# One level of Strassen's scheme in the second product of a feed-forward block, one core of a Trainium2

## Chip, cores and metric

The kernel runs on one core of one Trainium2 chip. The metric is device time in microseconds (us) of one launch. All arithmetic on values is in 32-bit floats.

## The reference

An mLSTM cell over q, k, v, three gates (4 batches, 8 heads, 768 steps, head dimension 40) gives x with 3072 rows and 320 columns; a feed-forward block follows:

```python
def _moe_ref(x, w_in, w_out) -> np.ndarray:     # x (3072, 320), w_in (320, 2048), w_out (2048, 320)
    h = np.maximum(x @ w_in, 0.0)
    return (h * h @ w_out).astype(np.float32)
```

The weights come as 64-bit floats and are rounded on the chip to 32 bits.

## The kernel before, in words

The 3072 rows are 24 tiles of 128 (4 batches of 6 chunks), s = 0 to 23. For each tile an attention step runs: `transposes` (k and q turned on TensorE, L342; ScalarE copies kT, VectorE copies qT, L346), `scores` (L355), `weighted` (VectorE multiplies the scores by the weights W, giving P_sb, L367), `attend` (hi, dC and hp on TensorE, L378, L385, L392; VectorE and POOL carry the state C on), `normalise` (eight or nine short VectorE operations, L418 to L428, that use the sigmoid of o_gate), and `turn_rows` (L437, copied to xT by ScalarE, L438). `weigh` makes W for the next tile: POOL masks A_bc (L312), ScalarE takes eight exponentials (L318).

Four tiles make a group of 512 rows, g = 0 to 5. For each group the feed-forward block has two stages of eight units each. A unit of the first product, `ffn1(g, p)`, makes two of the 16 blocks of d_ff: 128 x 512 results in PSUM (L452, L457; three banks h_ps), the relu on ScalarE into one of four r_sb buffers (L460), the square on VectorE into g2 (L461). A unit of the second product, `ffn2(g, j, part)`, runs 8 of the 16 matmuls of one tile of 128 rows, with 128 x 128 of g2 as the stationary operand and 320 columns of w_out streaming (L509), into one of two banks o_ps; after the second half ScalarE copies the 128 x 320 results (L515) and SP's queue writes them out (L517). TensorE runs a 32-bit matmul as two records in the trace.

The order of the work is written out by hand, and every engine takes its instructions in that order. A first part handles tiles 0 to 5, the rounding of the weights (`Rounding`, with buffers in the pool conv) and the first product of group 0. Then a loop runs over n = 8 to 95, sixteen units to a group (u = n mod 16): each unit is one of `ffn1` or `ffn2`, and the attention step of tile s = 4 + n // 4 is laid between four of them: `score` at n mod 4 = 0, `attend_on` at 1 (with the loads of tile s + 4 and of o_gate), `weigh_on` for the next tile at 2, `turn_rows` and the next tile's `transposes` at 3. At s = 7 and s = 15 ScalarE also takes the sigmoids of the next eight tiles of o_gate. The last two pieces of w_out are rounded at n = 8. From n = 80 on (group 5) no attention is left.

Of the kernel before, what the change touches and what calls it, by code (L numbers as in the profile page):

```python
# [9 lines left out]
F32 = mybir.dt.float32  # L10
# [4 lines left out]
ALU = mybir.AluOpType  # L15
PSUM = bass.MemoryType.PSUM

P = 128
# [11 lines left out]
def kernel(  # L30
# [21 lines left out]

    nc = tc.nc
    B, H, S, D = q.shape
    BH = B * H
    NB = S // P
    NT = B * NB
    PR = H // 2  # L60
    DP = 64
    D1 = D + 1
    DM = H * D
    DFF = moe_w_in.shape[1]
    NF = DFF // P
    NPAIR = NF // 2
    GT = 4
    NG = NT // GT
    W = GT * P
# [2 lines left out]

    consts = ctx.enter_context(tc.tile_pool(name="consts", bufs=1))
    ld = ctx.enter_context(tc.tile_pool(name="ld", bufs=2))
    conv = ctx.enter_context(tc.tile_pool(name="conv", bufs=2))
    prep = ctx.enter_context(tc.tile_pool(name="prep", bufs=2))
    work = ctx.enter_context(tc.tile_pool(name="work", bufs=2))
    xts = ctx.enter_context(tc.tile_pool(name="xts", bufs=2))
# [2 lines left out]
    ps_o = ctx.enter_context(tc.tile_pool(name="ps_o", bufs=2, space=PSUM))  # L81
    ctx.enter_context(tc.manual_schedule())
    first = ExitStack()
    gates = first.enter_context(tc.tile_pool(name="gates", bufs=1))

    A_d = nc.dram_tensor("a_rows", (BH, S), F32, kind="Internal").ap()

# [12 lines left out]
    w_out = consts.tile([P, NF, DM], F32)  # L100
# [31 lines left out]
    pieces = []  # L132
# [81 lines left out]
    rounding = Rounding()  # L214
# [36 lines left out]
    st = {}  # L251


    RUNS = ((0, 2), (2, 4), (4, 8), (8, 16), (16, 24))

    def load_parts(s):
        d = st.setdefault(s, {})
# [8 lines left out]
    def load_o(s):  # L266
        b, c = divmod(s, NB)
        r, (s0, s1) = next((r, (a, z)) for r, (a, z) in enumerate(RUNS) if a <= s < z)
        if s == s0:
            st["og", r] = ld.tile([P, 8, H, D], F32, name="og")  # L270
        og = st.setdefault(s, {})["og"] = st["og", r][:, s - s0]
        nc.sync.dma_start(og, o_gate[b, :, c * P : (c + 1) * P, :].rearrange("h p d -> p h d"))

    def sigmoid(s):
        nc.scalar.activation(st[s]["og"], st[s]["og"], AF.Sigmoid)
# [95 lines left out]
    def attend(s):  # L371
        b, c = divmod(s, NB)
        d = st[s]
        C = st.get("C")
        if c > 0:
            hi = ps_at.tile([P, H, D1], F32, name="hi", tag="at")
            for j in range(PR):
                nc.tensor.matmul(  # L378
                    hi[:, 2 * j : 2 * j + 2, :].rearrange("p h d -> p (h d)"), lhsT=d["qT"][:, j, :],
                    rhs=C[:, j].rearrange("p h d -> p (h d)"), start=True, stop=True,  # L380
                )
        if c + 1 < NB:
            dC = ps_at.tile([P, PR, 2, D1], F32, name="dC", tag="at")
            for j in range(PR):
                nc.tensor.matmul(  # L385
                    dC[:, j].rearrange("p h d -> p (h d)"),
                    lhsT=d["kq"][:, 0, 2 * j : 2 * j + 2, :].rearrange("p h d -> p (h d)"),
                    rhs=d["vw"][:, 2 * j : 2 * j + 2, :].rearrange("p h d -> p (h d)"), start=True, stop=True,
                )
        hp = d["hp"] = ps_at.tile([P, H, D1], F32, name="hp", tag="at")  # L390
        for h in range(H):
            nc.tensor.matmul(  # L392
                hp[:, h, :], lhsT=d["P"][h % 2][:, h // 2, :], rhs=d["va"][:, h, :], start=True, stop=True,
            )
        d["num"] = hp
        if c > 0:
            num = d["num"] = work.tile([P, H, D1], F32, name="num")
            nc.vector.tensor_tensor(  # L398
                num[:], hi[:], eA_T[:, b, c, :].unsqueeze(2).to_broadcast([P, H, D1]), op=ALU.mult,
            )  # L400
        if c + 1 < NB:
            Cn = work.tile([P, PR, 2, D1], F32, name="C_sb")
            nc.vector.tensor_tensor(Cn[:], dC[:], bdm[:], op=ALU.mult)  # L403
            if c > 0:
                Cd = work.tile([P, H, D1], F32, name="Cd")
                nc.gpsimd.tensor_tensor(
                    Cd[:], C[:].rearrange("p j i d -> p (j i) d"),
                    d["dec"][:].unsqueeze(2).to_broadcast([P, H, D1]), op=ALU.mult,
                )
                Cf = Cn[:].rearrange("p j i d -> p (j i) d")  # L410
                nc.gpsimd.tensor_tensor(Cf, Cf, Cd[:], op=ALU.add)  # L411
            st["C"] = Cn
# [29 lines left out]
    def ffn1(g, p):  # L442
        if p == 0 and g > 0:
            st["g2"] = ffn.tile([P, NF, W], F32, name="g2", bufs=1)
        xT = st["xT", g]
        hs = []
        for i in range(2):
            fb = 2 * p + i
            h = ps_h.tile([P, W], F32, name="h_ps")
            hs.append(h)  # L450
            for a in range(2):
                nc.tensor.matmul(  # L452
                    h[:], lhsT=w_in[:, a, fb * P : (fb + 1) * P], rhs=xT[:, a, :], start=(a == 0), stop=False,
                )
        for i in range(2):
            rows = slice(i * KR, (i + 1) * KR)
            nc.tensor.matmul(hs[i][:], lhsT=w_in2[rows, p, :], rhs=xT[rows, 2, :], start=False, stop=True)  # L457
        for i in range(2):
            r = ffn.tile([P, W], F32, name="r_sb", bufs=4)
            nc.scalar.activation(r[:], hs[i][:], AF.Relu)  # L460
            nc.vector.tensor_tensor(st["g2"][:, 2 * p + i, :], r[:], r[:], op=ALU.mult)  # L461
# [42 lines left out]
    def ffn2(g, j, part):  # L504
        if part == 0:
            st["o_ps"] = ps_o.tile([P, W], F32, name="o_ps")[:, :DM]
        o_ps = st["o_ps"]
        for fb in range(part * NF // 2, (part + 1) * NF // 2):
            nc.tensor.matmul(  # L509
                o_ps, lhsT=st["g2"][:, fb, j * P : (j + 1) * P], rhs=w_out[:, fb, :],  # L510
                start=(fb == 0), stop=(fb == NF - 1),
            )
        if part == 1:
            y = ffn.tile([P, DM], F32, name="y_sb")
            nc.scalar.copy(y[:], o_ps)  # L515
            t = g * GT + j
            nc.sync.dma_start(out[t * P : (t + 1) * P, :], y[:])  # L517


    def do(f, s):  # L520
        if 0 <= s < NT:
            f(s)

    def weigh_on(s):
        do(weigh, s)
        do(load_A, s + 2)
# [5 lines left out]
    def attend_on(s):  # L532
        do(attend, s)
        do(normalise, s)
        do(load, s + 4)
        if 4 <= s < 8:
            load_o(2 * s)
            load_o(2 * s + 1)
        elif 8 <= s < 16:
            load_o(s + 8)  # L540


    zeros = consts.tile([P, W], BF16)
# [47 lines left out]
    ffn = ctx.enter_context(tc.tile_pool(name="ffn", bufs=2))  # L591
# [4 lines left out]
    sigmoid(0)  # L596
    sigmoid(1)
    attend(0)
    rounding.step()
    normalise(0)  # L600
    load_o(2)
    load_o(3)
    attend(1)
    normalise(1)
    rounding.step()
# [12 lines left out]
    for u in range(8):  # L618
        s = 2 + u // 2
# [37 lines left out]
    NU = NPAIR + 2 * GT  # L657
    assert NU == 4 * GT
    for n in range(NPAIR, NU * NG):
        g, u = divmod(n, NU)  # L660
        s, at = GT + n // 4, n % 4
        if at == 0:
            do(score, s)
        if at == 1:
            attend_on(s)
        if at == 3:
            do(turn_rows, s)
            do(transposes, s + 1)
            if s in (7, 15):
                for r in range(s + 1, s + 9):  # L670
                    sigmoid(r)
        if u < NPAIR:
            ffn1(g, u)
        else:
            ffn2(g, *divmod(u - NPAIR, 2))
        while rounding.done < len(pieces):
            rounding.step()
        if at == 2:
            do(weigh_on, s + 1)

# [29 lines left out]
```

## Time and profile before

| | |
|---|---|
| Times of three runs, median | 608.71 us (607.28 to 608.88) |
| The profiled execution's own time | 608.44 us |
| Its span, first to last instruction | 606.7 us |
| Mean granted TensorE clock | 0.989 |
| L509 (second product) on TensorE | 768 records, 213.8 us |
| L452 and L457 (first product) on TensorE | 480 records, 192.1 us |

The trace names engines PE (TensorE matmuls), PEld (TensorE weight loads, which can lie beside matmuls), DVE (VectorE), ACT (ScalarE), POOL (GpSimd) and SP (the queue that issues most transfers). A group of instructions is shown as: line, engine, operation, output <- inputs, shapes, count | busy us, mean ns of one | idle time of the engine just before them, and what ended it. Ends of matmuls are modelled, so the distance between their starts tells more than their busy time. The chain of waits is followed back from the last instruction to whatever released each piece; a row of it in order of time is start, length, engine, tile, line and count.

### The profile page before, as it was taken

Reading aid. Unit: us, or ns where it says so; the run is one execution under the profiler, and the core shown is the slowest. Engines: PE = TensorE matmul, PEld = TensorE weight load, DVE = VectorE, ACT = ScalarE, POOL = GpSimd, SP = SyncE. Lnnn points to the kernel's source line nnn. Section 1 sums busy time; section 2 is a strip of 40 time slices with the busy share of each in tenths; the row PEclk is TensorE's granted clock in tenths of the full one; section 3 lists DMA queues with packets and bytes.
Section 4 is the critical chain, followed back from the end, with each engine's and each line's share of the span. In section 5 each row is a group of like instructions: output and inputs, shape, how many; then the busy total and the mean of one; then the engine's idle time right before and its main releaser. Section 6 shows DMA issues by size and latency. Waiting matters only on the chain.

```text
span 606.7 us, 7558 instructions
## 1 busy us (share of the span) xinstructions
PE 592.3 (98%) x2870; PEld 389.3 (64%) x2871; DVE 239.6 (39%) x468; ACT 192.4 (32%) x476; POOL 95.9 (16%) x113
## 2 busy tenths in 40 slices
PE   9979897999999999999999999999999999999997
PEld 5868776777645677645577655477755477733575
DVE  7688989712334322235323144322143431113100
ACT  3757567123351321132320524410214312022100
POOL 3345444202101110101021010101010110000000
PEclk9988998999999999999999999999999999999999
DMA  9898899615212143133143123122201000000000
GB/s 197 206 184 200 158 199 222 102 59 100 46 44 43 37 88 66 50 61 58 35 90 55 56 34 66 37 59 51 70 1 36 0 1 23 11 11 2 0 23 22
DMA packets 130901, 42.47 MB, mean 70 GB/s; under 512 B 101073, under 2 KB 127697, under 8 KB 130865
## 3 DMA queue, kind: packets, MB, share of 16 engines
q1 hardware_dynamic: 130768, 41.79, 33.2%
q8 instruction: 23, 0.38, 0.3%
q10 hardware_dynamic: 96, 0.20, 0.1%
q14 instruction: 14, 0.11, 0.1%
HBM read 37.95 MB, written 4.03 MB: 69 GB/s over the span
## 4 chain that ended last, share of the span: by engine, by line
PE 89%; DVE 6%; ACT 2%; issue 1%; POOL 1%; POOLq 0%; DVEq 0%; ACTq 0%
PE o_ps L509 35%; PE h_ps L452 23%; PE h_ps L457 7%; PE hp L392 6%; PE tp L355 3%; PE tp L342 3%; PE dC L385 3%; PE hi L378 2%; PE h_ps L476 2%; PE tp L437 1%; DVE mag L194 1%; DVE mag L195 1%; ACT W_sb L318 1%; PE idle L549 1%; POOL A_bc L312 1%
## 5 line engine op out<-in xcount | busy, mean ns | idle before, releaser
L509 PE MATMUL o_ps<-w_out,g 128*128 128x320 f32 x768 | 213.8, 435 | 0.0
L509 PEld LDWEIGHTS o_ps<-w_out,g 128*128 128x128 f32 x768 | 143.5, 190 | 57.9 <-issue 0.8
L452 PE MATMUL h_ps<-xT,w_in 128*128 128x512 f32 x320 | 146.9, 602 | 0.0
L461 DVE TENSOR_TENSOR g<-r_sb 128x512 f32<-128x512 f32 x80 | 51.7, 688 | 147.8 <-ACT r_sb L460 147.8
L452 PEld LDWEIGHTS h_ps<-xT,w_in 128*128 128x128 f32 x320 | 57.7, 190 | 69.9 <-issue 65.2
L460 ACT ACTIVATE r_sb<-h_ps 128x512 f32<-128x512 f32 x80 | 43.4, 595 | 162.6 <-PE h_ps L457 162.5
L515 ACT COPY y_sb<-o_ps 128x320 f32<-128x320 f32 x24 | 10.2, 425 | 185.8 <-PE o_ps L509 185.8
L318 ACT ACTIVATE W_sb<-A_bc,b_T 128x128 f32<-128x128 f32 x176 | 53.7, 391 | 7.9 <-POOL A_bc L312 7.9
L329 POOL TENSOR_TENSOR vw<-va,W_sb 128x328 f32<-128x328 f32 x20 | 14.9, 743 | 211.2 <-ACT W_sb L318 205.3
L367 DVE TENSOR_TENSOR P_sb<-tp,W_sb 128x512 f32<-128x512 f32 x46 | 29.6, 684 | 45.1 <-PE tp L355 43.0
L392 PE MATMUL hp<-va,P_sb 128*128 128x41 f32 x368 | 45.7, 286 | 0.0
L457 PE MATMUL h_ps<-xT,w_in 64*128 64x512 f32 x160 | 45.2, 641 | 0.0
L392 PEld LDWEIGHTS hp<-va,P_sb 128*128 128x128 f32 x368 | 44.6, 198 | 0.0
L346 DVE COPY qT<-tp 128x512 f32<-128x512 f32 x23 | 15.8, 687 | 70.2 <-PE tp L342 70.2
L411 POOL TENSOR_TENSOR C_sb<-C_sb,Cd 128x328 f32<-128x328 f32 x16 | 14.5, 906 | 138.1 <-DVE C_sb L403 137.8
L476 PE MATMUL h_ps<-xT,w_in 128*128 128x256 f32 x128 | 33.1, 415 | 3.0 <-ACT r_sb L495 1.2
L457 PEld LDWEIGHTS h_ps<-xT,w_in 64*128 64x128 f32 x160 | 12.0, 184 | 30.3 <-issue 30.3
L476 PEld LDWEIGHTS h_ps<-xT,w_in 128*128 128x128 f32 x128 | 26.1, 210 | 8.1 <-ACT r_sb L495 1.6
L355 PEld LDWEIGHTS tp<-qT,kT 40*128 40x128 f32 x384 | 24.1, 187 | 10.8 <-issue 6.8
L342 PE MATMUL tp<-ident,kq 128*128 128x128 f32 x192 | 26.6, 283 | 3.3 <-DVE num L398 3.3
L355 PE MATMUL tp<-qT,kT 40*128 40x128 f32 x384 | 27.1, 280 | 0.8 <-DVE qT L346 0.8
L342 PEld LDWEIGHTS tp<-ident,kq 128*128 128x128 f32 x192 | 23.0, 147 | 4.5 <-DVE num L398 3.8
(82 smaller groups left out, 468.8 us busy)
## 6 DMA issues: line engine op xcount, KB each, us to landing
A_bc<-a_rows SPq DMA_DIRECT2D x22, 512.0 KB, 3.9
raw<-in_moe_w_out_dram SPq DMA_DIRECT2D x16, 320.0 KB, 4.1
raw<-in_moe_w_in_dram SPq DMA_DIRECT2D x8, 512.0 KB, 5.1
kq<-in_k_dram SPq DMA_DIRECT2D x24, 160.0 KB, 4.0
kq<-in_q_dram SPq DMA_DIRECT2D x24, 160.0 KB, 4.4
va<-in_v_dram SPq DMA_DIRECT2D x24, 160.0 KB, 4.1
og<-in_o_gate_dram SPq DMA_DIRECT2D x24, 160.0 KB, 4.0
out_dram<-y_sb SPq DMA_DIRECT2D x24, 160.0 KB, 1.8
```

The source lines that it names most:

```text
L318: nc.scalar.activation(d["W"][:, i * n + h, :], A[i][:, h, :], AF.Exp, bias=b_T[:, b, c, i * n + h : i * n + h + 1],)
L342: nc.tensor.transpose(tp[:, j, :], d["kq"][:, i, 2 * j : 2 * j + 2, :].rearrange("p h d -> p (h d)"), ident[:],)
L355: nc.tensor.matmul(sc[i][:, j, :], lhsT=d["kT"][rows, j, :], rhs=d["qT"][rows, j, :], start=True, stop=True,)
L367: nc.vector.tensor_tensor(t, d["sc"][i], d["W"][:].rearrange("p (j two) t -> p j two t", two=2)[:, :, i, :], op=ALU.mult,)
L385: nc.tensor.matmul(dC[:, j].rearrange("p h d -> p (h d)"), lhsT=d["kq"][:, 0, 2 * j : 2 * j + 2, :].rearrange("p h d -> p (h d)"), rhs=d[" ...
L392: nc.tensor.matmul(hp[:, h, :], lhsT=d["P"][h % 2][:, h // 2, :], rhs=d["va"][:, h, :], start=True, stop=True,)
L452: nc.tensor.matmul(h[:], lhsT=w_in[:, a, fb * P : (fb + 1) * P], rhs=xT[:, a, :], start=(a == 0), stop=False,)
L457: nc.tensor.matmul(hs[i][:], lhsT=w_in2[rows, p, :], rhs=xT[rows, 2, :], start=False, stop=True)
L460: nc.scalar.activation(r[:], hs[i][:], AF.Relu)
L461: nc.vector.tensor_tensor(st["g2"][:, 2 * p + i, :], r[:], r[:], op=ALU.mult)
L476: nc.tensor.matmul(hs[i][:, n, :], lhsT=w_in[:, a, fb * P : (fb + 1) * P], rhs=xT[:, a, cols], start=(n == 0 and a == 0), stop=False,)
L509: nc.tensor.matmul(o_ps, lhsT=st["g2"][:, fb, j * P : (j + 1) * P], rhs=w_out[:, fb, :], start=(fb == 0), stop=(fb == NF - 1),)
```

## The change

For groups 1 to 5 the second product of a group, (512 rows x 2048) times (2048 x 320), is cut in two along each of its three dimensions: rows into tiles {0, 1} and {2, 3}, d_ff into blocks of even and odd number, the columns of w_out into 160 and 160. In place of the eight block products, seven are made (Winograd's form): P1 = A11 B11, P2 = A12 B21, P3 = S4 B22, P4 = A22 T2 (with its sign turned), P5 = S1 T0, P6 = S2 T1, P7 = S3 (B22 - B12), where A is g2 and B is w_out. They run for tile pairs (0, 2) and (1, 3), four units each.

- `sums` (VectorE): S1, S2, S3 (in place of A21) and S4 for two of the eight pairs of blocks at a time, four operations of 512 elements a partition; called at u = 2, 4, 6 and 8.
- `sums_of_weights` (VectorE): T0, T1, T2 at n = 10, 12, 14, and B22 - B12 in place of B12 at n = 18; 1280 elements a partition each.
- `product`: eight matmuls of 160 columns. Two banks X and Y take products by turns, and some of the additions are made by accumulating onto a product that is still there.
- `ffn2_fast`: four steps for a pair; step 3 has one product, the others two. Two ScalarE copies and five VectorE additions of 128 x 160 empty the banks into two rows y, which go out at steps 2 and 3.
- Memory: the pool conv is closed after the rounding, and S and T (pool late) take its place; o_gate is loaded in runs of four tiles in place of eight, at s = 8 to 19 for tile s + 4, and its sigmoids are taken in batches of four at s = 7, 11, 15 and 19; num and Cd have one buffer each.

Group 0 keeps `ffn2`. The core of the diff:

```diff
-    conv = ctx.enter_context(tc.tile_pool(name="conv", bufs=2))
...
+    brought = ExitStack()
+    conv = brought.enter_context(tc.tile_pool(name="conv", bufs=2, side="right"))
...
-    RUNS = ((0, 2), (2, 4), (4, 8), (8, 16), (16, 24))
+    RUNS = ((0, 2), (2, 4)) + tuple((s, s + 4) for s in range(4, NT, 4))
...
-            st["og", r] = ld.tile([P, 8, H, D], F32, name="og")
+            st["og", r] = ld.tile([P, 4, H, D], F32, name="og")
...
-            num = d["num"] = work.tile([P, H, D1], F32, name="num")
+            num = d["num"] = work.tile([P, H, D1], F32, name="num", bufs=1)
...
-                Cd = work.tile([P, H, D1], F32, name="Cd")
+                Cd = work.tile([P, H, D1], F32, name="Cd", bufs=1)
...
+    DH = DM // 2
+    W2 = W // 2
+    wo = w_out[:].rearrange("p (f two) d -> p f two d", two=2)
+    B11, B12 = wo[:, :, 0, :DH], wo[:, :, 0, DH:]
+    B21, B22 = wo[:, :, 1, :DH], wo[:, :, 1, DH:]
+    T = {}
+
+    def sums_of_weights(i):
+        if i < 3:
+            T[i] = late.tile([P, NPAIR, DH], F32, name=f"T{i}", bufs=1)[:]
+        if i == 0:
+            nc.vector.tensor_tensor(T[0], B12, B11, op=ALU.subtract)
+        elif i == 1:
+            nc.vector.tensor_tensor(T[1], B22, T[0], op=ALU.subtract)
+        elif i == 2:
+            nc.vector.tensor_tensor(T[2], B21, T[1], op=ALU.subtract)
+        else:
+            nc.vector.tensor_tensor(B12, B22, B12, op=ALU.subtract)
+
+    def sums(p0):
+        if p0 == 0:
+            st["S"] = [late.tile([P, NPAIR, W2], F32, name=f"S{n}", bufs=1) for n in (1, 2, 4)]
+        S1, S2, S4 = (t[:, p0 : p0 + 2] for t in st["S"])
+        g4 = st["g2"][:].rearrange("p (f two) t -> p f two t", two=2)[:, p0 : p0 + 2]
+        A11, A12, A21, A22 = (g4[:, :, i, n * W2 : (n + 1) * W2] for n in range(2) for i in range(2))
+        nc.vector.tensor_tensor(S1, A21, A22, op=ALU.add)
+        nc.vector.tensor_tensor(S2, S1, A11, op=ALU.subtract)
+        nc.vector.tensor_tensor(A21, A11, A21, op=ALU.subtract)
+        nc.vector.tensor_tensor(S4, A12, S2, op=ALU.subtract)
+
+    def product(to, lhsT, rhs, start=False):
+        for p in range(NPAIR):
+            nc.tensor.matmul(
+                to, lhsT=lhsT[:, p], rhs=rhs[:, p, :], start=(start and p == 0), stop=(p == NPAIR - 1),
+                skip_group_check=True,
+            )
+
+    def ffn2_fast(g, i, step):
+        if step == 0:
+            banks = [ps_o.tile([P, W], F32, name="o_ps") for _ in range(2)]
+            st["o2"] = banks if i == 0 else banks[::-1], [ffn.tile([P, DM], F32, name="y_sb") for _ in range(2)]
+        (X, Y), (y0, y1) = st["o2"]
+        g4 = st["g2"][:].rearrange("p (f two) t -> p f two t", two=2)
+        cols = [slice((i + 2 * n) * P, (i + 2 * n + 1) * P) for n in range(2)]
+        S1, S2, S4 = (t[:, :, i * P : (i + 1) * P] for t in st["S"])
+        X1, X5, Y6 = X[:, :DH], X[:, DH : 2 * DH], Y[:, :DH]
+        add = lambda to, a, b: nc.vector.tensor_tensor(to, a, b, op=ALU.add)
+        m1, u12, u22 = y1[:, :DH], y0[:, DH:], y1[:, DH:]
+        if step == 0:
+            product(X1, g4[:, :, 0, cols[0]], B11, start=True)
+            nc.scalar.copy(m1, X1)
+            product(Y6, S2, T[1], start=True)
+            add(u12, Y6, m1)
+        elif step == 1:
+            product(X1, g4[:, :, 1, cols[0]], B21)
+            nc.scalar.copy(y0[:, :DH], X1)
+            product(Y6, g4[:, :, 0, cols[1]], B12)
+            add(u22, Y6, m1)
+        elif step == 2:
+            product(X5, S1, T[0])
+            add(u22, u22, X5)
+            product(Y6, g4[:, :, 1, cols[1]], T[2])
+            add(m1, m1, Y6)
+            t = g * GT + i + 2
+            nc.sync.dma_start(out[t * P : (t + 1) * P, :], y1[:])
+        else:
+            product(X5, S4, B22)
+            add(u12, u12, X5)
+            t = g * GT + i
+            nc.sync.dma_start(out[t * P : (t + 1) * P, :], y0[:])
...
-        if 4 <= s < 8:
-            load_o(2 * s)
-            load_o(2 * s + 1)
-        elif 8 <= s < 16:
-            load_o(s + 8)
+        if 8 <= s < 20:
+            load_o(s + 4)
...
+        if n == NPAIR + 1:
+            brought.close()
+            late = ctx.enter_context(tc.tile_pool(name="late", bufs=1, side="right"))
+        if u == NPAIR and g > 0:
+            sums(NPAIR - 2)
         if at == 0:
             do(score, s)
         if at == 1:
             attend_on(s)
+        if n in (NPAIR + 2, NPAIR + 4, NPAIR + 6, NU + 2):
+            sums_of_weights((n - NPAIR) // 2 - 1 if n < NU else 3)
+        if 0 < u < NPAIR and u % 2 == 0:
+            sums(u - 2)
         if at == 3:
             do(turn_rows, s)
             do(transposes, s + 1)
-            if s in (7, 15):
-                for r in range(s + 1, s + 9):
+            if s % 4 == 3:
+                for r in range(s + 1, min(s + 5, NT)):
                     sigmoid(r)
         if u < NPAIR:
             ffn1(g, u)
+        elif g == 0:
+            ffn2(g, *divmod(u - NPAIR, 2))
+            while rounding.done < len(pieces):
+                rounding.step()
         else:
-            ffn2(g, *divmod(u - NPAIR, 2))
-        while rounding.done < len(pieces):
-            rounding.step()
+            ffn2_fast(g, *divmod(u - NPAIR, 4))
```

## The prediction

> **What bounds the kernel now.** I read the page of the profile first: busy shares, the 40 slices, and the chain of work that ended last.
>
> ```profile
> PE 592.3 (98%) x2870; PEld 389.3 (64%) x2871; DVE 239.6 (39%) x468; ACT 192.4 (32%) x476; POOL 95.9 (16%) x113
> ...
> PE   9979897999999999999999999999999999999997
> ...
> DVE  7688989712334322235323144322143431113100
> ...
> PEclk9988998999999999999999999999999999999999
> ...
> PE 89%; DVE 6%; ACT 2%; issue 1%; POOL 1%; POOLq 0%; DVEq 0%; ACTq 0%
> PE o_ps L509 35%; PE h_ps L452 23%; PE h_ps L457 7%; PE hp L392 6%; PE tp L355 3%; PE tp L342 3%; PE dC L385 3%; PE hi L378 2%; PE h_ps L476 2%; PE tp L437 1%; DVE mag L194 1%; DVE mag L195 1%; ACT W_sb L318 1%; PE idle L549 1%; POOL A_bc L312 1%
> ```
>
> TensorE is busy for 98% of the span and is 89% of the chain; the largest entry, 35%, is the line that the change replaces, the second product L509. A busy TensorE may only be waiting with a matmul in flight, so I asked next for the stretches: the second table gives each engine's busy time (and instruction count) in a first-product stage, in a second-product stage, and in the last group.
>
> ```profile
> core 0: us, PE busy (x) PEld busy (x) DVE busy (x) ACT busy (x) POOL busy (x), PEclk, DMA share, GB/s
> 203.97:249.46 45.49, 45.49 (x240) 34.46 (x238) 11.88 (x25) 9.29 (x27) 4.75 (x5) 1.00 0.32 68
> 249.46:297.50 48.04, 48.04 (x210) 24.76 (x212) 18.06 (x36) 14.56 (x37) 4.79 (x6) 1.00 0.25 49
> 568.70:606.70 38.00, 34.63 (x128) 24.15 (x128) 1.29 (x2) 2.79 (x6) 0.00 (x0) 1.00 0.05 18
> ```
>
> The second-product stage of group 1 (the first row) has no idle TensorE at all, at a granted clock of 1.00, while VectorE works 11.88 of 45.49 us. Whether its time is really streaming shows in the pitch of its matmuls, which the chain in order of time gives (start, us, how many):
>
> ```profile
> 55.65 3.46 PE h_ps L476 x16
> ...
> 204.86 4.50 PE o_ps L509 x16
> ...
> 211.11 1.75 PE hp L392 x16
> ...
> 221.88 0.87 PE tp L342 x8
> 222.75 4.31 PE o_ps L509 x16
> ...
> 457.86 3.44 PE h_ps L452 x8
> 461.30 1.06 PE h_ps L457 x4
> ...
> 568.68 34.66 PE o_ps L509 x128
> ```
>
> A record of 512 columns takes 3.44/8 = 430 ns, one of 320 takes 4.31/16 = 269.4, one of 256 takes 3.46/16 = 216.3. The line through the first two is 0.836 ns per column and 1.8 ns; it gives 216 at 256, as measured. So these stages are bound by the columns streamed, and a stage that streams fewer columns ends earlier, as long as nothing else comes last. The floor on the other side is the weight load that every record brings: hp streams 41 columns only and still takes 1.75/16 = 109 ns, the transposes 0.87/8 = 109 ns.
>
> **The change, part by part.** The durations that its terms need stand in the groups of instructions (count, then busy us and mean ns):
>
> ```profile
> L509 PE MATMUL o_ps<-w_out,g 128*128 128x320 f32 x768 | 213.8, 435 | 0.0
> ...
> L461 DVE TENSOR_TENSOR g<-r_sb 128x512 f32<-128x512 f32 x80 | 51.7, 688 | 147.8 <-ACT r_sb L460 147.8
> L460 ACT ACTIVATE r_sb<-h_ps 128x512 f32<-128x512 f32 x80 | 43.4, 595 | 162.6 <-PE h_ps L457 162.5
> ...
> L515 ACT COPY y_sb<-o_ps 128x320 f32<-128x320 f32 x24 | 10.2, 425 | 185.8 <-PE o_ps L509 185.8
> ...
> L367 DVE TENSOR_TENSOR P_sb<-tp,W_sb 128x512 f32<-128x512 f32 x46 | 29.6, 684 | 45.1 <-PE tp L355 43.0
> ```
>
> *Removed.* L509 has 768 records: 24 row tiles, 16 blocks of d_ff, two records to a matmul. Five of six groups change: 640 records x 269.4 ns = 172.4 us, all on the path.
>
> *Added on TensorE.* Each of those groups has two pairs of row tiles, seven products each, 8 matmuls to a product, two records to a matmul: 2 x 7 x 8 x 2 = 224 records of 160 columns, 1120 in all. No row has 160 columns. The line above gives 0.836 x 160 + 1.8 = 135.6 ns. From below it is bounded by half of 269.4, 134.7; from above by a load that is not hidden at all, 109 + 134.7 = 244 ns. I take 135.6: the 256-column row lies on the line and the 109 ns floor is 26 ns under it, so the load still fits behind the stream. 1120 x 135.6 = 151.9 us, again all on the path. Difference: 172.4 - 151.9 = 20.5 us off.
>
> *Starts of products.* A start can cost more than the pitch: the x16 after the scores took 4.50 us, that after the transposes 4.31, so 0.19 us at the first start of a stage. Each group now has 14 products, each waiting for a bank to be emptied. A bank change in the old stage costs next to nothing (34.66 - 8 x 4.31 = 0.18 us over the whole last group, its first start included). Bounds: 0 and 14 x 5 x 0.19 = 13 us; I take 1 us, by the nearest row, the bank changes.
>
> *Emptying the banks.* Per pair two ScalarE copies of 160 columns and five VectorE additions with one operand in PSUM. From L515 (320, 425 ns) and L460 (512, 595) a copy of 160 is an estimated 283 ns. A PSUM operand on VectorE is in L367 and in the row below, 328 columns: 1.03 ns per column, so an estimated 322 ns at 160, 50 x 0.322 = 16 us.
>
> ```profile
> L398 DVE TENSOR_TENSOR num<-hi,eA_T 128x328 f32<-128x328 f32 x20 | 9.9, 495 | 29.4 <-PE hi L378 29.4
> ...
> L275 ACT ACT_TABLE_LOAD x5 | 6.4, 1283 | 0.1
> ```
>
> The banks alternate X, Y, X, Y: while one is emptied the other takes a product of 16 x 135.6 ns = 2.17 us, against 0.32 or 0.28 us of emptying, so the cost is nothing. The cover shrinks to nothing only if VectorE is over 1.8 us behind at that moment.
>
> *Block sums of g2.* Four tensor_tensor of 512 elements for every two pairs of blocks, 16 a group, 80 in all, 688 ns each by L461: 55 us of VectorE. Those of u = 2, 4, 6 stand in the first-product stage, where VectorE is busy 18.06 of 48.04 us; with 12 x 0.688 = 8.3 us it comes to 26. What queues behind them are the squares, which wait for the relu of the same unit, a whole unit (3.44 + 1.06 = 4.5 us) later; the four sums take 2.75. Cost nothing; without that cover the four r_sb buffers still let VectorE lag nearly two units. Those of u = 8 are the tight ones; the old course of that place, group 1, is:
>
> ```profile
> 203.80 1.06 PE L355 MATMUL tp<-qT,kT 40*128 40x128 f32 x16
> ...
> 204.63 1.29 DVE L461 TENSOR_TENSOR g<-r_sb 128x512 f32<-128x512 f32 x2 [3.96 <-ACT r_sb L460]
> 204.79 4.57 PE L509 MATMUL o_ps<-w_out,g 128*128 128x320 f32 x16
> 205.84 1.28 DVE L367 TENSOR_TENSOR P_sb<-tp,W_sb 128x512 f32<-128x512 f32 x2
> ...
> 212.69 2.14 POOL L312 TENSOR_SCALAR_AFFINE_SELECT A_bc<-A_bc 128x1024 f32<-128x1024 f32 x2
> ...
> 213.84 1.01 DVE L421 TENSOR_TENSOR dm<-dm,num 128x8 f32<-128x8 f32 x1
> ...
> 215.48 0.49 DVE L427 TENSOR_TENSOR x_sb<-x_sb,dm 128x320 f32<-128x320 f32 x1
> ```
>
> The last squares end at 205.92. Now S1 ends at 206.6, S2 at 207.3, S3 and S4 at 208.7, and only then come the two P_sb, at 209.4 and 210.05 instead of 207.1. TensorE starts the first product at 204.9; the second starts at 207.0 and needs the last quarter of S2 at 208.7, 1.4 us after it is there. Then hi runs to about 210.1, dC needs the bank that the first P_sb frees (there at 209.4), and hp needs the second (210.05) at about 211. So nothing is late, by 0.7 to 1 us. In the last group there are no scores: the second product wants the last quarter of S2 at 568.68 + 2.17 + 12 x 0.136 = 572.5, and S2, by the same course, is there at about 572.0. In step 1 the normalising of the attention step goes ahead of the additions on VectorE: it ends about 3.1 us after hp (L427 at 215.97, hp at 212.86), before the 4.3 us of the two products that follow hp, so the addition after them starts on time.
>
> *Sums of w_out.* Three times 1280 elements in group 0's second product and one at u = 2 of group 1, 0.684 + 768 x 0.00103 = 1.47 us each, 6 us in all, a whole stage ahead of their use, which is the end of group 1's first product. The tiles take the memory of the rounding buffers, so the first sum waits for the last rounding on POOL, two units before it: nothing. VectorE in all: 239.6 + 55 + 16 + 6 = 317 us, 54% of the new time.
>
> *Moved and split.* The o_gate loads of tiles 12 to 23 are issued at most four steps ahead; each still has two units between its issue and its sigmoid, as the loads of tiles 14 and 15 have now. Four sigmoid batches of 4 replace two of 8: two more batches, two table loads each (sigmoid, then exp), 4 x 1.28 = 5.1 us of ScalarE, which is busy 9.29 of 45.49 us in such a stage; they stand behind the last copy that the next tile needs. Nothing; if a relu were held up, the three h_ps banks would give it a unit. Single buffers for num and Cd serve one engine each, which runs in order: nothing. The rows y go out four per group as before; the second one of a pair now stands on SP's queue behind the next load of A_bc, which waits for ScalarE's exponentials; these start one step (over 4 us) earlier than the addition that the row waits for. A row buffer is taken again over 4 us after its transfer is issued, and that takes:
>
> ```profile
> out_dram<-y_sb SPq DMA_DIRECT2D x24, 160.0 KB, 1.8
> ```
>
> The end of the kernel, one emptying and one such transfer, stays.
>
> *Sum.* The profiled execution took 608.44 us (span 606.7), 0.27 under the median of 608.71. 608.44 - 20.5 + 1.0 = 588.9; on the median 589.2. I predict 589.
>
> **The rivals.** *A. The weight load is not hidden at 160 columns: slower.* Place: every record of the new products. 1120 loads take the place of 640, each behind a stream of 135 ns where 269 hid it. The break-even pitch is 172.4 / 1120 = 154 ns, so 18 ns of the 109 showing per record turn the gain to nothing; all of it gives 1120 x 244 = 273 us and a time of 608.4 - 172.4 + 273 = 709. Against it: if loads stood outside the streams, the 320-column record would take 109 + 267 = 376 ns, not 269.4; and the transposes show a load-bound pitch of 109 with no extra for the swap. For it: no row has a stream so little longer than its load. The Trainium skill says, in "TensorE: Matmul & The Clock Gate", Part 3 ("What overlaps and what doesn't"), that a weight load runs beside matmuls in flight only when their row groups differ; by that rule all of these loads, full height, would stand outside, which is this rival's 709. The trace contradicts it at 320 columns. Chance 0.07.
>
> *B. Starts of products show.* Every product begins with a wait, and each costs the 0.19 us of a first start: 13 us in place of 1, so 601; half of them, 595. For it: 14 waits a group in place of four. Against it: the 0.18 us of the whole last group. Chance 0.10.
>
> *C. P_sb comes late at u = 8.* The sums stand ahead of it on VectorE, with 0.7 to 1 us to spare. The timeline shows a tensor_tensor of 8 elements taking 1.01 us, begun under POOL's mask of A_bc; the line's median is 0.173:
>
> ```profile
> L421 DVE TENSOR_TENSOR dm<-dm,num x20: 172/173/1199, 29.1 to 518.8; 128x8 f32<-128x8 f32 x20
> ```
>
> The Trainium skill ("SBUF — State Buffer", "Who interferes with whom") states that a VectorE instruction with two SBUF inputs contends with a GpSimd one that reads SBUF; the sums are of that kind, so by it they can be held up too. If each of the four lost 0.84 us, P_sb would be 3.4 us later and TensorE would wait some 2.5 us in four groups: 599. Against it: POOL's mask starts at 212.69 there, after the sums. Chance 0.07.
>
> *D. The gain is not there*, because denser weight loads lower the granted clock by the 3.4% that 20.5 of 608 us are. All stages above show 1.00. Time 608, chance 0.02.
>
> **How the numbers follow.** The forecast (587 to 591.5) has 0.74, B 0.10, C 0.07, A 0.07, D 0.02. The low end is the 134.7 ns bound without any start: 608.44 - 172.4 + 150.9 = 587. Upwards the range takes in half of B and most of C: 597. With A, D and the upper part of B and C outside, some 0.15 is left out. A measurement of this kernel tells some 0.3%, 1.8 us, from no change. Faster: 0.74 + 0.10 + 0.07 = 0.91; the same 0.02 (D); slower 0.07 (A).
>
> **What would show it.** Right: 1120 records of 160 columns at a pitch near 136 ns, so each pair's products cost 15.2 us; second-product stages about 4 us shorter, first-product stages as long as before; TensorE still busy throughout; VectorE near 317 us; no wait of TensorE for S, T or a bank in the list of waits. Wrong: a pitch over 140 ns in a product's middle (A), gaps at product starts (B), TensorE waiting for P_sb at u = 8 (C), a clock under 1.00 (D), or first-product stages that grow by what VectorE was given.

## The result, and the profile after

The changed kernel took 588.54 us (median of 4 runs, 587.59 to 588.78) against 608.49 for the kernel before in the same comparison: a ratio of 0.9672, 95% interval 0.9655 to 0.9690. The forecast was 589.

The profiled execution took 587.59 us, its span is 585.8. Its page, the same parts as of before:

```profile
PE 572.5 (98%) x3351; PEld 421.3 (72%) x3351; DVE 311.6 (53%) x602; ACT 195.6 (33%) x480; POOL 96.1 (16%) x113
...
PE   9979998999999999999999999999999999999997
...
DVE  8687989934276553256562356652346653225611
...
PEclk9987989999999999999999999999999999999999
...
PE 84%; DVE 7%; ACT 3%; issue 2%; POOL 2%; DMA 2%; SPq 0%; POOLq 0%; DVEq 0%; ACTq 0%
PE o_ps L564 26%; PE h_ps L454 24%; PE h_ps L459 7%; PE o_ps L511 6%; PE hp L394 5%; PE tp L357 3%; PE tp L344 3%; PE hi L380 2%; PE dC L387 2%; DMA kq<-in_q_dram 2%; DVE mag L196 2%; ACT W_sb L320 2%; DVE mag L197 2%; PE tp L439 1%; POOL A_bc L314 1%
```

TensorE is as full as before, VectorE went from 39% to 53%, and the second product (now L564 for five groups and L511 for group 0) from 35% of the chain to 32%. The stretches that answer to the three shown of before, with the same columns (group 1's second product, the first product after it, the last group):

```profile
203.65:245.32 41.67, 41.67 (x336) 41.08 (x335) 17.38 (x39) 11.15 (x32) 4.76 (x5) 1.00 0.34 71
245.32:293.49 48.17, 48.14 (x207) 24.50 (x207) 25.97 (x49) 16.41 (x39) 4.80 (x6) 1.00 0.27 53
551.96:585.80 33.84, 30.63 (x225) 30.38 (x224) 7.10 (x16) 2.25 (x6) 0.00 (x0) 0.99 0.06 20
```

The second-product stage is about 4 us shorter and still without idle TensorE; the first-product stage is as long as before though VectorE does 8 us more in it. The chain in order of time gives the pitch and the whole account:

```profile
108.74 4.50 PE o_ps L511 x16
...
203.65 4.54 PE o_ps L564 x32
...
211.69 8.77 PE o_ps L564 x64
...
221.66 2.18 PE o_ps L564 x16
...
551.96 30.64 PE o_ps L564 x224
```

A record of 160 columns takes 2.18/16 = 136 ns; in the last group 30.64 us replace 34.66, 4.0 us, and five such stages make 20.1. From the first record of the second product to the last it is now 551.96 + 30.64 - 108.74 = 473.9 us. Before, the chain had its first such record at 110.11 and its last group as quoted, 568.68 + 34.66 - 110.11 = 493.2. So this part lost 19.4 us. The rest of the difference of the spans, 1.5 us, lies almost all ahead of it, where the start came at 108.74 in place of 110.11. The last unit of the first product of group 0, first before and then after, shows why:

```profile
102.33 5.14 PE h_ps L476 x16
```

```profile
102.65 3.46 PE h_ps L478 x16
```

These are the same 16 records of 256 columns. In the profile of before the granted clock was 0.67 on average in these 5.14 us, at 0.50 from about 102.6 to 106; in that of the changed kernel it was 1.00.

### The profile page after: what moved, and what is told of

Read it like the earlier page. It is cut to its first block, busy times and chain, and to the rows that moved or that the text cites. A ratio compares the mean times of both kernels' runs of the same rounds, so it can differ in the third digit from the quotient of the medians.

```text
span 585.8 us, 8684 instructions
## 1 busy us (share of the span) xinstructions
PE 572.5 (98%) x3351; PEld 421.3 (72%) x3351; DVE 311.6 (53%) x602; ACT 195.6 (33%) x480; POOL 96.1 (16%) x113
## 4 chain that ended last, share of the span: by engine, by line
PE 84%; DVE 7%; ACT 3%; issue 2%; POOL 2%; DMA 2%; SPq 0%; POOLq 0%; DVEq 0%; ACTq 0%
PE o_ps L564 26%; PE h_ps L454 24%; PE h_ps L459 7%; PE o_ps L511 6%; PE hp L394 5%; PE tp L357 3%; PE tp L344 3%; PE hi L380 2%; PE dC L387 2%; DMA kq<-in_q_dram 2%; DVE mag L196 2%; ACT W_sb L320 2%; DVE mag L197 2%; PE tp L439 1%; POOL A_bc L314 1%
## 5 line engine op out<-in xcount | busy, mean ns | idle before, releaser
L564 PE MATMUL o_ps<-w_out,g 128*128 128x160 f32 x480 | 70.1, 302 | 0.0
L564 PEld LDWEIGHTS o_ps<-w_out,g 128*128 128x128 f32 x480 | 65.8, 190 | 1.7 <-issue 0.8
L564 PE MATMUL o_ps<-T,S 128*128 128x160 f32 x320 | 46.7, 299 | 0.0
L564 PEld LDWEIGHTS o_ps<-T,S 128*128 128x128 f32 x320 | 44.5, 190 | 0.0
L580 DVE TENSOR_TENSOR y_sb<-y_sb,o_ps 128x160 f32<-128x160 f32 x30 | 9.6, 321 | 53.3 <-PE o_ps L564 53.3
L413 POOL TENSOR_TENSOR C_sb<-C_sb,Cd 128x328 f32<-128x328 f32 x16 | 14.5, 908 | 136.8 <-DVE C_sb L405 136.6
L511 PE MATMUL o_ps<-w_out,g 128*128 128x320 f32 x128 | 35.8, 435 | 0.0
L511 PEld LDWEIGHTS o_ps<-w_out,g 128*128 128x128 f32 x128 | 23.8, 190 | 9.4
```

The lines of the kernel that those rows point to most:

```text
L511: nc.tensor.matmul(o_ps, lhsT=st["g2"][:, fb, j * P : (j + 1) * P], rhs=w_out[:, fb, :], start=(fb == 0), stop=(fb == NF - 1),)
L564: nc.tensor.matmul(to, lhsT=lhsT[:, p], rhs=rhs[:, p, :], start=(start and p == 0), stop=(p == NPAIR - 1), skip_group_check=True,)
```

## The experiments

The theory: TensorE streams columns at a pitch fixed by their number, the weight load lies behind the stream, and all that the change adds on VectorE and ScalarE lies beside it. The rivals: a load that shows, starts of products, P_sb late at u = 8, and, new, that the first part became faster by the move of the buffers.

**Two halves of 160 columns, nothing else** (from the kernel before):

```diff
-                o_ps, lhsT=st["g2"][:, fb, j * P : (j + 1) * P], rhs=w_out[:, fb, :],
-                start=(fb == 0), stop=(fb == NF - 1),
...
+            cuts = (0, DM) if g == 0 else (0, DM // 2, DM)
+            for c0, c1 in zip(cuts, cuts[1:]):
...
+                    o_ps[:, c0:c1], lhsT=st["g2"][:, fb, j * P : (j + 1) * P], rhs=w_out[:, fb, c0:c1],
+                    start=(fb == 0 and c0 == 0), stop=(fb == NF - 1), skip_group_check=True,
```

> The kernel before, but for groups 1 to 5 each matmul of the second product is made as two of 160 columns with the same stationary block: 1280 records of 160 columns in place of 640 of 320, no sums, nothing left out. Theory (columns bound, the load lies behind the stream): 1280 x 135.8 - 640 x 269.0 = +1.7 us, so 610.2 from 608.5, at a pitch of 136 ns. Rival (part of the weight load shows at 160 columns, and the change gained from something else): for each 10 ns of load that shows, 12.8 us more; with all 109 ns, 750.

Measured: 609.95 us, ratio 1.0031 (1.0019 to 1.0042), 1.6 us above the 608.36 of before beside it. Its last group in the chain:

```profile
569.96 34.98 PE o_ps L511 x256
```

34.98/256 = 136.6 ns with twice as many loads, 0.32 us more than the 34.66 of 128 wide records. The load is hidden at 160 columns, and cutting the columns alone gains nothing: all of the gain is the eighth block product that is not made (five groups of 32 records of 136 ns, 21.8 us, against 609.95 - 588.54 = 21.4).

**Narrower products:**

```diff
-            product(X1, g4[:, :, 1, cols[0]], B21)
+            product(X1, g4[:, :, 1, cols[0]], B21, n=96)
...
-            product(Y6, g4[:, :, 0, cols[1]], B12)
+            product(Y6, g4[:, :, 0, cols[1]], B12, n=128)
...
-            product(Y6, g4[:, :, 1, cols[1]], T[2])
+            product(Y6, g4[:, :, 1, cols[1]], T[2], n=112)
...
-            product(X5, S4, B22)
+            product(X5, S4, B22, n=144)
```

> The changed kernel with four of the seven products narrowed (columns left out): A12 B21 streams 96 columns, S3 (B22 - B12) 128, A22 T2 112, S4 B22 144. Theory (the pitch is the larger of the stream and a load floor of about 109 ns): 96, 112 and 128 columns all at 109 ns, 144 at 122; per pair 16 x (3 x 26.8 + 13.6) = 1.5 us less, 15 us in all, so 573.5. Rival 1 (streams alone set the pitch): 82, 95, 109 and 122 ns, so 567. Rival 2 (the starts and ends of products set the pace, not the pitch): 588.5.

This kernel leaves out the last 64, 32, 48 and 16 columns of four products. Measured: 574.61 us, ratio 0.9450 (0.9434 to 0.9466). TensorE in the last group; the x32 row holds a product of 96 columns and one of 128, and distances between starts count:

```profile
546.24 3.73 PE L564 MATMUL o_ps<-w_out,g 128*128 128x96 f32 x32
549.81 2.34 PE L564 MATMUL o_ps<-T,S 128*128 128x160 f32 x16
551.99 1.93 PE L564 MATMUL o_ps<-T,g 128*128 128x112 f32 x16
553.76 2.14 PE L564 MATMUL o_ps<-w_out,S 128*128 128x144 f32 x16
555.73 2.34 PE L564 MATMUL o_ps<-w_out,g 128*128 128x160 f32 x16
```

96 and 128 columns together, on average: (549.81 - 546.24)/32 = 111.6 ns; 112: 1.77/16 = 110.6; 144: 1.97/16 = 123; 160: 2.18/16 = 136. So the floor is there at about 111 ns, a little above the 109 assumed, and 144 columns still lie on the streaming line. Both rivals are out.

**Sums of g2 in group 1 alone:**

```diff
-            sums(NPAIR - 2)
+            g == 1 and sums(NPAIR - 2)
...
-            sums(u - 2)
+            g == 1 and sums(u - 2)
```

> The changed kernel with the block sums of g2 made in group 1 alone (left out in groups 2 to 5, where S keeps the values of group 1): 64 operations and 44 us of VectorE less. Theory (all sums lie beside TensorE's work): 588.5, within 0.6 us. Rival (TensorE waits for VectorE somewhere): faster by what it waits; from the list of waits at most 1 us, from contention on SBUF perhaps 3 to 5 us.

This kernel leaves out the sums of groups 2 to 5. Measured: 588.79 us, against 588.54 with all sums. 40 us of VectorE (271.4 in place of 311.6) are worth nothing.

**More sums in the first product's stages:**

```diff
+        for _ in range(4 if p0 < NPAIR - 2 else 0):
+            nc.vector.tensor_tensor(S4, A12, S2, op=ALU.subtract)
```

> The changed kernel with S4 written five times at u = 2, 4 and 6 (the same values): 60 more operations, 38 us more of VectorE, in the first product's stages. Theory (the squares may lag nearly two units, and P_sb, qT and x stand with over a us to spare there): 588.5, within 1 us. Rival (VectorE at some 60% of the time becomes the bound of those stages): up to 2.5 us for each of the 15 places, 626.

Measured: 588.20 us, with VectorE at 354.7 us, 60% of the span. Both sides of this cover are now shown: nothing to gain by less, nothing lost by 43 us more (60 operations of 0.69 us).

**More sums at u = 8**, the same lines with `p0 == NPAIR - 2` and four, three and two repeats:

> The changed kernel with S4 written five times in place of once at u = 8 (the same values): four more operations of 512 elements on VectorE ahead of P_sb, 2.5 us. Theory (P_sb has 0.95 us to spare before dC and 1.2 us before hp at this place): TensorE waits about 1.6 us, 2.1 where there is no hi, once in each of groups 1 to 4, so 588.5 + 6.8 = 595.3. Rival (VectorE's place in the order decides nothing, only its sum of work): 588.5.

Measured: 612.36 us (607.62 to 615.85 in five runs), ratio 1.0068 (1.0051 to 1.0084) to the kernel before: slower than it, 24 us above the change, where 7 were expected. The waits came nearly as worked out: TensorE waits 1.97 us for P_sb in three groups and 1.88 in the fourth, 7.8 us where 6.8 were expected. What followed was not in the theory. The stretches around the wait in group 1, in the profiled execution (615.85 us), TensorE's column first, PEclk third from the end:

```profile
208.90:212.10 3.20, 3.19 (x26) 3.03 (x24) 3.10 (x6) 0.29 (x1) 0.00 (x0) 1.00 0.00 0
212.10:214.06 1.96, 0.00 (x1) 0.04 (x1) 1.93 (x4) 0.00 (x0) 0.00 (x0) 1.00 0.00 0
214.06:216.03 1.97, 1.97 (x10) 1.97 (x10) 1.09 (x3) 0.00 (x0) 0.00 (x0) 0.50 0.00 0
216.03:219.37 3.34, 3.34 (x17) 3.34 (x17) 0.50 (x1) 0.00 (x0) 2.60 (x3) 0.50 0.63 98
219.37:222.00 2.63, 2.63 (x11) 2.63 (x12) 2.09 (x7) 0.00 (x0) 0.37 (x1) 0.50 0.62 106
222.00:226.00 4.00, 4.00 (x23) 4.00 (x23) 0.00 (x0) 2.19 (x8) 0.00 (x0) 0.71 0.07 12
```

After the wait the granted clock is 0.50 from 214.06 to 222 and on average 0.71 up to 226, some 10 us at half speed: hp takes 3.34 us in place of 1.75. The mean granted clock of the whole run is 0.961 against 0.985; 614.1 x 0.039 - 585.8 x 0.015 = 15 us are lost that way, twice as much as by the waits. Two smaller doses were to show where this sets in:

> The changed kernel with S4 written three times at u = 8 (the same values): two more operations, 1.44 us, ahead of P_sb. TensorE should wait 0.5 us in three groups and 1.0 in the one without hi, 2.5 us. Theory (what the run with four more lost beyond its waits, 15 us, is the granted clock at half for some 8 us after a wait of 2 us, and a short wait doesn't bring it down): 591. Rival (any wait at this place brings the clock down): 591 + 4 x 3.9 = 607.

> As the last one, with S4 written four times: three more operations, 2.16 us, so waits of 1.2 us in three groups and 1.7 in the fourth, 5.3 us: 594 if the clock stays up, 609 if it comes down in all four, and a value between them if the length of the wait is near the point. No theory of mine says which.

Measured: 594.0 us with two more, 3 us above the 591 of the theory and far from the 607 of the rival, and 601.05 with three, between the two values named. In the profile with two, the waits are 0.4 to 0.5 us and the clock fell after one of the four; in the one with three, about 1.2 us, and it fell after three of four. One place with three more, the wait and what follows, then the half-clock stretch with two:

```profile
208.98:210.24 1.26, 0.01 (x2) 0.04 (x1) 1.26 (x3) 0.00 (x0) 0.00 (x0) 1.00 0.00 0
210.24:212.90 2.66, 2.66 (x24) 2.66 (x25) 1.58 (x4) 0.00 (x0) 0.82 (x1) 1.00 0.16 26
212.90:216.30 3.40, 3.40 (x15) 3.40 (x15) 2.98 (x7) 0.00 (x0) 2.14 (x3) 0.50 1.19 170
```

```profile
396.50:400.00 3.50, 3.50 (x15) 3.50 (x15) 1.58 (x6) 0.00 (x0) 0.00 (x0) 0.51 0.67 114
```

So the mechanism of rival C is real: VectorE's place in the order decides there, with about 1 us to spare, and the price of missing it is the wait plus a clock at half for 3.4 us and more. The rival that any wait brings the clock down is out, and so is the theory that a short one never does; no clear threshold in the length of the wait shows.

**The same bank twice in step 2:**

```diff
-            product(X5, S1, T[0])
-            add(u22, u22, X5)
             product(Y6, g4[:, :, 1, cols[1]], T[2])
             add(m1, m1, Y6)
+            product(X5, S1, T[0])
+            add(u22, u22, X5)
```

> The changed kernel with the two products of step 2 swapped: Y again right after Y, so that the product cannot start until the addition that empties Y is done. Nothing is left out. Theory (turning from bank to bank is what hides the emptying; without it the addition of 0.32 us, the way there and back and a load show): 0.6 us at each of the ten places, so 594.5. Rival (the emptying is short enough not to matter either way): 588.5.

Measured: 597.73 us, ratio 0.9824 (0.9809 to 0.9839), 9.2 us above the change. The last group, with what TensorE waited for:

```profile
568.70 2.44 PE L564 MATMUL o_ps<-T,g 128*128 128x160 f32 x16 [0.42 <-DVE y_sb L580]
570.97 2.34 PE L564 MATMUL o_ps<-T,S 128*128 128x160 f32 x16
...
573.79 2.44 PE L564 MATMUL o_ps<-w_out,S 128*128 128x160 f32 x16 [0.48 <-DVE y_sb L580]
```

The mechanism is as expected, the count was not: the swap also puts X behind X at step 3, which the transposes of the next tile cover except in the last group and once in group 4 (a wait of 0.16 us). In the chain of group 1 the two steps take 9.45 us (213.23 to 222.68) against 8.77, 0.7 a place; 13 places make 9.

**kT of four tiles on VectorE:**

```diff
-            (nc.scalar.copy if i == 0 or s == 0 else nc.vector.tensor_copy)(d[n][:], tp)
+            (nc.scalar.copy if (i == 0 and (s < 9 or s % 4 != 1)) or s == 0 else nc.vector.tensor_copy)(d[n][:], tp)
```

> The changed kernel with VectorE copying kT for tiles 9, 13, 17 and 21, whose copy on ScalarE stands behind a reload of the exp table and the exponentials. Nothing is left out. Theory (the scores of these four tiles wait 0.3 us for kT): four waits go, 1.2 us, so 587.3. Rival (they would wait for qT next): 588.5.

Measured: 586.93 us. In the list of waits (who waited for whom, us, times, longest) of the kernel before, then of the changed kernel:

```profile
PEld tp L355 <- ACT kT L346: 1.7, 2, 0.9
```

```profile
PEld tp L357 <- ACT kT L348: 3.4, 4, 0.9
```

Two such waits became four, and with this edit none is left in the list. What stands ahead of one of the two new waits in the changed kernel:

```profile
263.20 1.28 ACT L320 ACT_TABLE_LOAD   x1
...
267.31 0.58 ACT L348 COPY kT<-tp 128x512 f32<-128x512 f32 x1
...
267.94 0.97 PEld L357 LDWEIGHTS tp<-qT,kT 40*128 40x128 f32 x16 [0.86 <-ACT kT L348]
```

The load of the table comes first, then the eight exponentials, then kT. The 0.86 us are idle time of the weight loads; in the chain such scores take 1.16 us in place of 0.89, so TensorE loses 0.27 us a time. The medians differ by 1.6 us, just under what a run can tell; the waits themselves are read from the trace.

**Old second product in the new layout** (the calls of `sums`, `sums_of_weights` and `ffn2_fast` taken out, `ffn2` for all groups):

> The changed kernel's memory, o_gate loads, sigmoid batches and single buffers, with the old second product in all groups and no sums: nothing is left out. Theory (the gain is the shorter stream alone, and the two added reloads of the exp table cost 0.3 us each): 608.5 + 0.6 = 609.1. Rival (the first part became faster by the move of the buffers or the loads, as the start of the second product 1.4 us earlier in the one profile may say): 607.1.

Measured: 608.89 us, ratio 1.0013 (0.9999 to 1.0027). Its chain:

```profile
103.54 5.99 PE h_ps L478 x16
...
112.16 4.50 PE o_ps L511 x16
...
571.33 34.66 PE o_ps L511 x128
```

571.33 + 34.66 - 112.16 = 493.8 us, 0.6 above the kernel before, as two more reloads cost. The time is that of the theory and not the rival's 607.1. The profiled execution of this kernel started its second product at 112.16, with the memory and loads of the changed kernel, whose own started at 108.74; before, it was 110.11. The unit ahead of it took 5.99 us at a mean clock of 0.58, where it took 3.46 at 1.00 and 5.14 at 0.67. So the 1.4 us by which the changed kernel's profile started earlier lie in where the clock stood at half in that execution, and are no effect of the change.

**A part of group 0 too**, with kT as above. The core of the edit:

```diff
+        for i in {NPAIR + 1: (0,), NPAIR + 2: (1, 2), NPAIR + 4: (3,)}.get(n, ()):
+            sums_of_weights(i)
+        if n == NPAIR + 2:
+            sums_of_pair(0)
...
+        if n == NPAIR + 3:
+            sums_of_pair(4)
...
-        elif g == 0:
-            ffn2(g, *divmod(u - NPAIR, 2))
+        elif g == 0 and u < NPAIR + 4:
+            ffn2(g, 2 * ((u - NPAIR) // 2), u % 2)
```

> The changed kernel with kT of tiles 9, 13, 17 and 21 copied by VectorE, and with the scheme in half of group 0 too: tiles 0 and 2 by the old second product, then tiles 1 and 3 as a pair by seven products; the sums of w_out at n = 9, 10 and 12, the block sums for that pair at n = 10 and 11. Nothing is left out. Theory (TensorE is the bound in group 0's second product as well): 64 records of 269.0 ns become 112 of 135.8, 2.0 us, on top of 1.6 by the run with kT alone: 585.0. Rival (group 0's stage, with VectorE still rounding weights, has no room for 11 us of sums ahead of the products): 587 or more.

Measured: 585.62 us, ratio 0.9628 (0.9610 to 0.9646), the fastest of the kernels that leave nothing out. Group 0's second product stands in its chain as:

```profile
110.72 4.50 PE o_ps L511 x16
...
133.12 4.54 PE o_ps L575 x32
...
141.17 8.77 PE o_ps L575 x64
...
151.13 2.18 PE o_ps L575 x16
153.31 1.09 PE tp L357 x16
154.40 3.63 PE h_ps L454 x8
```

From 110.72 to 154.40 it is 43.7 us, against 154.59 - 108.74 = 45.9 in the changed kernel, so 2.2 us less where 2.0 were expected. The pair runs at the known pitch, so there was room for the sums on VectorE.

## Why the prediction was right, point by point

The two large terms held. The pitch at 160 columns was worked out as 135.6 ns from rows of 320 and 512 columns and is 136; 19.4 us less between the first and the last record stand against 20.5 - 1.0 = 19.5. That they agree so closely is partly luck: five second-product stages lost 20.1, so the starts cost 0.4 us more than in the old kernel and not 1.0, and the 0.6 allowed too much is what two waits that the prediction put at nothing took (below). The halves show that the price of halving the columns is what the line says, 1.6 us measured for 1.7, and the narrow products show the floor where rival A would begin: 111 ns, which the line reaches at about 130 columns, 30 fewer than are streamed. One reading of the prediction doesn't carry what it was used for: by its own line 128 columns stream in 0.836 x 128 + 1.8 = 109 ns, so the transposes' 109 ns can't tell a load from a stream; only hp's 41 columns could.

The covers held as well, and the runs show them rather than the account alone: fewer sums and more sums in the first product's stages change nothing, and emptying a bank, 0.32 us on VectorE (0.29 on ScalarE), shows only when the next product wants the same bank. All starts of products of the last group together cost 30.64 - 224 x 0.1356 = 0.27 us, against 0.18 in the old last group, so rival B is out.

One step failed, a small one: of the added sigmoid batches the prediction said that they stand behind the last copy that the next tile needs and cost nothing. The sigmoids do; the reload of the exp table that follows does not. It stands ahead of the next exponentials, and kT of the tile after stands behind those, so the scores wait. Two more waits of 0.3 us came, 0.6 us in all.

The place called tight was tight. In the changed kernel, group 1:

```profile
207.28 1.28 DVE L369 TENSOR_TENSOR P_sb<-tp,W_sb 128x512 f32<-128x512 f32 x2
...
208.88 1.06 PE L387 MATMUL dC<-vw,kq 128*128 128x82 f32 x8
```

The first P_sb was there at about 207.93, 0.95 us before dC wanted its bank. The cause that rival C named did not arise: the 60 sums written to S took 679 to 694 ns each, and none of the 80 block sums ran beside an instruction of POOL, so what such an overlap costs them is not shown. What the prediction had too low is C's price. It took the wait alone, 2.5 us in each of four groups, 599 (outside the 597 that the range ends at, though the range was said to take in most of C); four operations more at this place, with waits of 2 us, cost 24 us and take back the whole gain. With that price C would have ended on the side of slower, at the same small chance.

## What to carry to other kernels

Where TensorE has no idle time, work out the pitch of the new shape from rows of other shapes, and check it against the floor of the weight load: down to about 130 columns of 32-bit data a block scheme costs no load time here. Put the additions where VectorE has a stage's slack, let products turn from bank to bank, and look for the one place where the sums stand in front of something that TensorE needs soon. A wait of TensorE there is not priced by its length: add what the clock loses after it.

## What the runs showed of the hardware that was not expected

The granted clock fell to half after short waits of TensorE at u = 8: after 1.9 to 2.0 us in all four places, for 7 to 10 us; after 1.2 us in three of four; after 0.4 to 0.5 us in one of four. The pages show it in their 40 slices, for four, three and two operations more and then for the run with the same bank twice (the slices up to the eighth are the first part):

```profile
PEclk9988998999999969999979999989999998999999
```

```profile
PEclk9978998999999989999979999989999999999999
```

```profile
PEclk9997999999999999999999999989999999999999
```

```profile
PEclk9997989999999999999999999999999999999999
```

The Trainium skill ("TensorE: Matmul & The Clock Gate", "Why this matters for your kernels") warns of idle gaps above some 3 us between bursts; here 2 us were enough in all four places. Waits of about 0.5 us between full products (the run with the same bank twice) never brought it down: its page shows no drop of the clock after the first part. What follows the wait is different there: at u = 8 it is dC and hp, 82 and 41 columns at a pitch of 109 to 112 ns, of which the stream takes 70 and 36 ns (an estimate by the prediction's line).

But neither the length of the wait nor the work behind it decides alone. In the first part of the kernel before, TensorE waited 0.81 us ahead of the transposes at 82.66 and the clock stayed at 1.00; in the changed kernel it waited 0.82 us ahead of the same transposes at 82.98, and 3.4 us at 0.50 followed. At 102 it was the other way round: after 2.10 us the clock fell for 3.5 us before, and after 2.07 us it stayed up in the changed kernel. The stretches at half after u = 8 last about 3.4, 6.8 or 10.2 us, which speaks for a fixed period. Whether the place of the wait in such a period decides, and whether the narrow matmuls count, was not tried and stays open.
